# Reordering one pair of heads in a fused attention and soft-mixture kernel: transposes in another PSUM ring, V products and denominators at other places

## The chip, the cores and the metric

The kernel runs on one core of one Trainium2 chip. The metric is the device time of one execution in microseconds (us). A core has a matrix engine (PE, with its weight loads shown apart as PEld), a vector engine (DVE), an activation engine (ACT), a general engine (POOL) and a sync engine (SP). Each works through its own queue in order, and they meet at semaphores. PE writes its results to PSUM, which has eight banks of 512 float32 values in each of 128 partitions; DVE and ACT empty them.

## The reference

```python
def _attn_ref(q, k, v):                       # 8 batches, 12 heads, 448 tokens, 64 channels
    scores = scale * np.matmul(q, k.transpose(0, 1, 3, 2))
    m = np.max(scores, axis=-1, keepdims=True)
    e = np.exp(scores - m)
    attn = e / (np.sum(e, axis=-1, keepdims=True) + np.exp(-m) + 1e-09)
    return np.matmul(attn, v).astype(np.float32)

def _moe_ref(x, phi, w1, w2):                 # x: 3584 x 768, phi: 768 x 32, 8 experts of 4 slots
    logits = x @ phi
    d = np.exp(logits - logits.max(0, keepdims=True))
    d /= d.sum(0, keepdims=True) + 1e-09
    slot_input = (d.T @ x).reshape(E, S_per_e, D)
    for e in range(E):
        slot_out[e] = np.maximum(slot_input[e] @ w1[e], 0.0) @ w2[e]
    c = np.exp(logits - logits.max(1, keepdims=True))
    c /= c.sum(1, keepdims=True) + 1e-09
    return (c @ slot_out).astype(np.float32)
```

The attention's output, with its heads side by side, is the x of the second part. The dispatch weights d are normalised over all 3584 rows, so the experts can begin only when the last head is done.

## The kernel before

The 96 heads are worked as 48 pairs of heads of one batch: one head lies in partitions 0 to 63, the other in 64 to 127. Six pairs make a batch; three pairs make a group, whose q, k and v are loaded together. The loop of line 647 goes over the pairs s; each has two half chunks, y = 0 and y = 1, and hs = 2s + y counts them. Everything is written out by hand in the order in which each engine is to run it: the program is not reordered.

For one pair the work is this.

- `T(n)` (L237): 28 transposes of 64x64 turn q and k, six pairs ahead, into one PSUM tile. One copy, on ACT (L256) or on DVE (L258), brings them to one of seven buffers.
- `A` and `A1` (L269, L288): products of q against k, seven PSUM tiles a pair, three to four pairs ahead. DVE takes the maximum of each row (L278, L286, L293).
- `W2`, `W3` (L296, L306), once per group of three pairs: the maxima are turned (L300 to L303) and copied by ACT (L308), and ACT takes exp(-m) of them (L312, L315).
- `AB(n, i)` (L348), key blocks i = 0, 1, 2 of 128 keys: k against q (`scores`, L360), minus the maximum by a second product into the same bank (`less`, L363), and the exponential on ACT (L365). One tile of the row maxima (`A1`, L292) runs ahead of it and one behind. `Bk(n, 3, 1)` (L319) does the fourth block of 64 keys (L338, L341, exponential L344), with the `A` of L284 inside.
- `AV(n, i, qs)` (L386, L398): the exponentials against V, 65 columns a product; the last column of V is one, which gives the denominators. Query blocks 0 to 2 are wide products (24 a pair), query block 3 is narrow (8 a pair, half of the output partitions each). All 32 add up in one PSUM bank.
- `N1(n)` (L404): that bank is copied to SBUF, by ACT (L410) for pairs 0 to 43 and DVE after that. `N2(n)` (L413): DVE adds exp(-m) to the denominators (L419) and takes the reciprocal (L420), then POOL (pairs 0 to 43) or DVE multiplies (L424, L428, L429). `PX(n)` (L443) turns the result (L450) and ACT copies it (L456).
- `P(b)` (L463): per batch, the logits, their maxima, their exponentials and the running sum of the slots' inputs, cut into steps that the table `post` spreads over the half chunks of the next batch but one: logits (L476, L489, L493) in a half chunk y = 0, their transposes (L501, L503, and a subtraction on POOL, L508) in y = 1, the running maximum (L513, L514, L516) in y = 0, exponentials (L525, L530) in y = 0, slot sums (L544, L535, L558) in y = 1, and one more turn (L549) in y = 1.

PSUM is three rings of banks: psA with three (rows' maxima, the steps of P, and the transposes of pairs 8 and later), psB with four (scores for the exponentials, W2, PX, and the transposes of pairs 0 to 7), psV with one (the V products). A tile is given the bank that the ring's oldest tile left, and PE waits until that one has been read.

The order of a half chunk before, away from the start and the end:

- y = 0: blocks 0 and 1; the wide V products of key blocks 2 and 3 of the pair before; a step of P where there is one; the narrow V products of the pair before; N1 (and N2, where DVE does it all).
- y = 1: block 2; block 3; the transposes of pair s + 6; W2 and W3 in one pair of three; wide V products of key blocks 0 and 1; a step of P; PX of pair s - 2; N2.

Loads and the copies of V by POOL (L377) follow at the end of a pair. After the loop come the last pair's rest, the experts (L751 to L849) and the output (L851 to L866).

## Time and profile before

| | |
|---|---|
| time, three runs | 303.99, 305.38, 305.58 us; median 305.38 us |
| the profiled execution's own time | 304.84 us |
| its span, first to last instruction | 303.1 us |
| mean granted PE clock | 0.948 |
| busy: PE, DVE, ACT, POOL | 275.1, 254.4, 249.3, 184.8 us |
| row maxima on DVE (L293) | 254 of 616 ns mean, 139.9 us |
| exponentials on ACT (L365) | 272 of 576 ns mean, 131.2 us |
| copies of transposes, ACT (L256) and DVE (L258) | 20 of 924 ns, 27 of 616 ns |
| V products on PE (L398) | 1536, 64.5 us |

A line of a view has the engine, the line of the program, the operation, what it writes and reads, its shapes, and how many there were. In the timeline the first two numbers are the start and the duration of a run of like instructions, in microseconds from the first instruction; brackets at the end give the idle time of the engine before it and what ended that. The mean of a row is one instruction's own length; instructions of one engine overlap, so the starts tell more of the pace than the lengths. The window from 33 to 224 us is the part in which the transposes are still running beside everything else.

### The profile page before, as it was taken

Reading aid. Unit: us, or ns where it says so; the run is one execution under the profiler, and the core shown is the slowest. Engines: PE = TensorE matmul, PEld = TensorE weight load, DVE = VectorE, ACT = ScalarE, POOL = GpSimd, SP = SyncE. Lnnn points to the kernel's source line nnn. Section 1 sums busy time; section 2 is a strip of 40 time slices with the busy share of each in tenths; the row PEclk is TensorE's granted clock in tenths of the full one; section 3 lists DMA queues with packets and bytes.
Section 4 is the critical chain, followed back from the end, with each engine's and each line's share of the span. In section 5 each row is a group of like instructions: output and inputs, shape, how many; then the busy total and the mean of one; then the engine's idle time right before and its main releaser. Section 6 shows DMA issues by size and latency. Waiting matters only on the chain.

```text
span 303.1 us, 12159 instructions
## 1 busy us (share of the span) xinstructions
PE 275.1 (91%) x5097; PEld 159.3 (53%) x5097; DVE 254.4 (84%) x590; ACT 249.3 (82%) x551; POOL 184.8 (61%) x336
## 2 busy tenths in 40 slices
PE   7998999999999999999999999999999998994800
PEld 3344656566665666556656575656665455541100
DVE  7889999999999999989999999999999566447900
ACT  3567999999999999989999999999999995345800
POOL 8691986969596869866877778696747652000000
PEclk9599999999999999999999999999999999998555
DMA  7999899999999999999999999999846999909995
GB/s 130 143 149 202 124 206 208 203 199 174 186 179 195 163 198 161 200 190 155 117 202 144 191 195 208 159 204 205 138 54 107 133 151 247 336 29 347 440 410 233
DMA packets 49384, 57.69 MB, mean 190 GB/s; under 512 B 2865, under 2 KB 41521, under 8 KB 48945
## 3 DMA queue, kind: packets, MB, share of 16 engines
q0 software_dynamic: 45280, 42.29, 90.5%
q1 hardware_dynamic: 4048, 14.62, 12.2%
q8 instruction: 40, 0.66, 0.8%
q14 instruction: 16, 0.12, 0.1%
HBM read 88.18 MB, written 14.16 MB: 338 GB/s over the span
## 4 chain that ended last, share of the span: by engine, by line
PE 66%; DVE 15%; ACT 10%; issue 3%; POOL 0%; DVEq 0%; POOLq 0%
PE ps_av L398 14%; PE ps_a L292 9%; PE ps_b L360 7%; DVE R L293 6%; PE ps_b L363 6%; PE ps_t L252 6%; PE ps_b L338 4%; ACT R L344 3%; PE ps_x L450 2%; PE ps_b L341 2%; PE ps_o L803 2%; ACT R L256 2%; DVE R L278 2%; PE ps_so L774 2%; PE ps_h L758 2%
## 5 line engine op out<-in xcount | busy, mean ns | idle before, releaser
L293 DVE TENSOR_REDUCE R<-ps_a 128x1 bf16<-128x448 f32 x254 | 139.9, 616 | 5.6 <-PE ps_a L292 5.1
L365 ACT ACTIVATE R<-ps_b 128x448 bf16<-128x448 f32 x272 | 131.2, 576 | 0.5 <-PE ps_b L363 0.2
L292 PE MATMUL ps_a<-R 64*128 64x448 bf16 x254 | 82.8, 352 | 0.3 <-DVE R L278 0.2
L360 PE MATMUL ps_b<-R 64*128 64x448 bf16 x272 | 74.7, 353 | 1.1
L363 PE MATMUL ps_b<-mT,sel 64*128 64x448 bf16 x272 | 71.3, 350 | 0.1
L424 POOL TENSOR_TENSOR R<-ubuf,rec 128x384 bf16<-128x384 f32 x44 | 36.2, 822 | 50.0 <-DVE rec L420 21.8
L398 PEld LDWEIGHTS <-R 128*128 128x128 bf16 (+1 forms) x1536 | 50.6, 101 | 27.8 <-issue 23.7
L398 PE MATMUL ps_av<-R 128*128 128x65 bf16 (+1 forms) x1536 | 64.5, 196 | 0.0
L344 ACT ACTIVATE R<-ps_b 128x448 bf16<-128x448 f32 x64 | 36.1, 581 | 3.5 <-PE ps_b L341 3.5
L252 PEld LDWEIGHTS <-R 64*64 64x64 bf16 x1344 | 29.7, 111 | 12.4 <-issue 4.6
L456 ACT CAST R<-ps_x 128x512 bf16<-128x512 f32 x47 | 28.1, 599 | 6.5 <-PE ps_x L450 6.5
L252 PE MATMUL ps_t<-ident,R 64*64 64x64 bf16 x1344 | 30.9, 195 | 0.6
L286 DVE TENSOR_REDUCE R<-ps_a 128x1 bf16<-128x448 f32 x48 | 29.7, 619 | 0.6 <-PE ps_a L284 0.6
L363 PEld LDWEIGHTS <-sel 64*128 64x128 bf16 x272 | 21.8, 94 | 15.3 <-issue 5.5
L292 PEld LDWEIGHTS <-R 64*128 64x128 bf16 x254 | 23.8, 94 | 11.0 <-issue 1.0
L410 ACT COPY ubuf<-ps_av 128x455 f32<-128x455 f32 x44 | 25.1, 571 | 0.6 <-POOL R L429 0.4
L256 ACT COPY R<-ps_t 128x896 bf16<-128x896 bf16 x20 | 18.5, 924 | 5.5 <-PE ps_t L252 5.1
L338 PE MATMUL ps_b<-R 64*64 64x448 bf16 (+1 forms) x112 | 22.0, 378 | 0.0
L278 DVE TENSOR_REDUCE R<-ps_a 128x1 bf16<-128x448 f32 x34 | 19.0, 618 | 2.5 <-PE ps_a L275 2.2
L341 PE MATMUL ps_b<-mT,sel 64*64 64x448 bf16 (+1 forms) x112 | 20.8, 357 | 0.0
L429 POOL TENSOR_TENSOR R<-ubuf,rec 128x128 bf16<-128x128 f32 x44 | 17.5, 398 | 3.7
L360 PEld LDWEIGHTS <-R 64*128 64x128 bf16 x272 | 17.3, 94 | 4.7 <-issue 0.3
(139 smaller groups left out, 442.6 us busy)
## 6 DMA issues: line engine op xcount, KB each, us to landing
W<-in_moe_w_dram POOLq DMA_DIRECT2D x22, 768.0 KB, 10.1
R<-in_v_dram POOLq DMA_DIRECT2D x32, 192.0 KB, 4.8
out_dram<-W SPq DMA_DIRECT2D x2, 2688.0 KB, 12.1
R<-in_q_dram POOLq DMA_DIRECT2D x14, 336.0 KB, 7.8
R<-in_k_dram POOLq DMA_DIRECT2D x14, 336.0 KB, 8.7
wd<-in_moe_w_dram POOLq DMA_DIRECT2D x8, 384.0 KB, 9.9
R<-wd SPq DMA_DIRECT2D x8, 384.0 KB, 7.8
R<-in_moe_w_dram POOLq DMA_DIRECT2D x2, 768.0 KB, 8.0
```

The source lines that it names most:

```text
L252: nc.tensor.transpose(ps[r, a, c:c + 64], src[r, pl, tok * D:(tok + 1) * D], ident[r, r])
L286: nc.vector.reduce_max(top(n, i), ps[:, 0:S], axis=AX.X)
L292: nc.tensor.matmul(ps[:, 0:S], t[r, 0, i * 128:(i + 1) * 128], t[r, 1, :], start=True, stop=True)
L293: nc.vector.reduce_max(top(n, i, hl), ps[:, 0:S], axis=AX.X)
L338: nc.tensor.matmul(outs[hl], t[rs[hl], 1, cols], t[rs[hl], 0, :], start=True, stop=False)
L344: nc.scalar.activation(e, p[:, 0:S], AF.Exp, scale=scale)
L360: nc.tensor.matmul(ps[hl][:, 0:S], t[rs[hl], 1, cols], t[rs[hl], 0, :], start=True, stop=False)
L363: nc.tensor.matmul(ps[hl][:, 0:S], sel[rs[hl], pl:pl + 1].to_broadcast([64, 128]), mT[mg(n)][rs[hl], :], start=False, stop=True)
L365: nc.scalar.activation(e[:, hl, :], ps[hl][:, 0:S], AF.Exp, scale=scale)
L398: nc.tensor.matmul(o, eT[n, i, hl][:, qc], vp[g % 2][:, 2 * pl + hl, i, 0:W65], start=(i == 0 and u == 0 and hl == 0), stop=(i == 3), skip ...
L424: eng.tensor_mul(x[:, 0:3, c:c + 128].rearrange("p i (h d) -> p i h d", h=2), u[:, 0:6, 0:D].rearrange("p (i h) d -> p i h d", h=2), rec[: ...
L456: nc.scalar.copy(xT[:, pb, :], pss[0])
```

## The change

Five things change, all of them in order or place; no arithmetic is added or left out.

1. The transposes take their PSUM tile from psB for all pairs, not from psA for pair 8 and later. The copy goes to ACT for the second pair of a group (pl == 1), before for the first.
2. In y = 1 the transposes come between block 2 and block 3, before behind block 3.
3. In y = 0 the eight narrow V products come between block 0 and block 1, before at the end of the half chunk. N1 follows the wide V products at once, ahead of the step of P.
4. N2 becomes N2a (the sum, L419) and N2b (reciprocal and multiplications). Where POOL multiplies, N2a stands between the transposes and block 3, and N2b behind block 3, ahead of W2, W3 and the step of P; before, both came at the end of the half chunk behind PX.
5. In y = 1 the step of P comes before the wide V products, before after them.

The first two and a half pairs (`early`) keep their own order of blocks.

```diff
--- before.py
+++ after.py
@@ -236,13 +236,12 @@
 
         def T(n):
             g, pl = divmod(n, NP)
-            tp, tg = (psB, "b") if n < 8 else (psA, "a")
             t = qk_t[n % NQK]
-            ps = tp.tile([128, 2, S], BF16, tag=tg, name="ps_t")
+            ps = psB.tile([128, 2, S], BF16, tag="b", name="ps_t")
             for a in range(2):
                 if n == 0 and a:
                     nc.scalar.copy(t[:, 0, :], ps[:, 0, :])
-                    ps = tp.tile([128, 2, S], BF16, tag=tg, name="ps_t")
+                    ps = psB.tile([128, 2, S], BF16, tag="b", name="ps_t")
                 src = nat["qk"[a], g]
                 for tok in range(7):
                     for hl in range(2):
@@ -252,7 +251,7 @@
                         nc.tensor.transpose(ps[r, a, c:c + 64], src[r, pl, tok * D:(tok + 1) * D], ident[r, r])
             if n == 0:
                 nc.vector.tensor_copy(t[:, 1, :], ps[:, 1, :])
-            elif n < 8 or pl == 0:
+            elif n < 8 or pl == 1:
                 nc.scalar.copy(t, ps)
             else:
                 nc.vector.tensor_copy(t, ps)
@@ -410,13 +409,17 @@
             (nc.scalar.copy if on_pool(n) else nc.vector.tensor_copy)(u, src)
             us[n] = u
 
-        def N2(n):
-            g, pl = divmod(n, NP)
+        recs = {}
+
+        def N2a(n):
+            recs[n] = psm.tile([128, 7], F32, tag="rec", name="rec", bufs=3)
+            nc.vector.scalar_tensor_tensor(recs[n], us[n][:, :, D], 1e-9, ec[mg(n)][:, n % NP, :],
+                                           op0=ALU.add, op1=ALU.add)
+
+        def N2b(n):
             b, pb = divmod(n, PB)
-            u = us[n]
+            u, rec = us[n], recs[n]
             eng = nc.gpsimd if on_pool(n) else nc.vector
-            rec = psm.tile([128, 7], F32, tag="rec", name="rec", bufs=3)
-            nc.vector.scalar_tensor_tensor(rec, u[:, :, D], 1e-9, ec[mg(n)][:, pl, :], op0=ALU.add, op1=ALU.add)
             nc.vector.reciprocal(rec, rec)
             x = xb[b % 2]
             c = pb * 128
@@ -656,46 +659,51 @@
                     Bk(s, 2 * y + 1)
                     warm(int(hs < 2), S)
                     As(1)
-                elif s < NPAIR:
-                    AB(s, 2 * y)
-                    if y:
-                        Bk(s, 3, 1)
-                    else:
-                        AB(s, 1)
+                elif y == 0:
+                    AB(s, 0)
+                    for i in range(4):
+                        AV(s - 1, i, [3])
+                    AB(s, 1)
+                else:
+                    AB(s, 2)
+                    if s < NPAIR - 6:
+                        T(s + 6)
+                    if on_pool(s - 1):
+                        N2a(s - 1)
+                    Bk(s, 3, 1)
                 if hs < 5:
                     T(hs + 3)
                 if y == 0:
-                    if 0 <= s - 1:
+                    if s:
                         for i in (2, 3):
                             AV(s - 1, i, range(3))
+                        if early:
+                            for i in range(4):
+                                AV(s - 1, i, [3])
+                        N1(s - 1)
+                        if not on_pool(s - 1):
+                            N2a(s - 1)
+                            N2b(s - 1)
                 else:
-                    if 2 <= s < NPAIR - 6:
-                        T(s + 6)
+                    if s and on_pool(s - 1):
+                        if early:
+                            N2a(s - 1)
+                        N2b(s - 1)
                     g = (s + 1) // 3
                     if (s + 1) % 3 == 0 and g < NG:
                         W2(g + 1)
                         W3(g + 1)
-                    if s < NPAIR:
-                        for i in (0, 1):
-                            AV(s, i, range(3))
-                if 2 * s + y in post:
-                    post[2 * s + y]()
+                if hs in post:
+                    post[hs]()
+                if y:
+                    for i in (0, 1):
+                        AV(s, i, range(3))
                 if hs == 2 * (NPAIR - 2) + 1:
                     nc.vector.reduce_max(fold, ident.rearrange("p (i s) -> p s i", i=4), axis=AX.X)
                 if y and 0 <= s - 2 < NPAIR - 2 and s - 2 != n6:
                     PX(s - 2)
                 if hs == 2 * n6 + 4:
                     PX(n6)
-                if y == 0:
-                    if 0 <= s - 1:
-                        for i in range(4):
-                            AV(s - 1, i, [3])
-                        N1(s - 1)
-                        if not on_pool(s - 1):
-                            N2(s - 1)
-                else:
-                    if 0 <= s - 1 and on_pool(s - 1):
-                        N2(s - 1)
                 As(last_)
                 if hs == 1:
                     W2(1)
@@ -733,7 +741,8 @@
         AV(n, 3, range(4))
         load_second(0, 4)
         N1(n)
-        N2(n)
+        N2a(n)
+        N2b(n)
         PX(n - 1)
         last[0]()
         last[1]()
```

## The prediction

> **What bounds the kernel now.** The granted clock and the engines' busy time by window come first: they say whether the attention part has one bound.
>
> ```profile
> 33.00:224.00 191.00, 188.86 (x3823) 118.00 (x3818) 181.82 (x421) 183.53 (x421) 146.44 (x260) 1.00 1.14 180
> ```
>
> The columns are the stretch, then busy microseconds of PE, PEld, DVE, ACT and POOL, the granted clock, the DMA share and GB/s. The clock is full (1.00). DVE is idle for 191.00 - 181.82 = 9.2 us and ACT for 191.00 - 183.53 = 7.5 us. Three engines run almost full, so no reordering that leaves their work alone can win much more than the 7.5 us. PE's 188.86 says little: records of matmuls overlap, and a matmul that starts late hides behind the end of the one before. So I read PE by starts, in the timeline of one pair and the beginning of the next:
>
> ```profile
> 141.80 0.55 PE L360 MATMUL ps_b<-R 64*128 64x448 bf16 x2
> 142.00 0.54 PE L363 MATMUL ps_b<-mT,sel 64*128 64x448 bf16 x2
> 142.19 0.54 PE L292 MATMUL ps_a<-R 64*128 64x448 bf16 x2
> 142.38 0.80 PE L360 MATMUL ps_b<-R 64*128 64x448 bf16 x2
> 142.84 0.53 PE L363 MATMUL ps_b<-mT,sel 64*128 64x448 bf16 x2
> 143.04 0.35 PE L292 MATMUL ps_a<-R 64*128 64x448 bf16 x1
> 143.32 0.79 PE L398 MATMUL ps_av<-R 128*128 128x65 bf16 x20
> ...
> 144.71 0.38 PE L338 MATMUL ps_b<-R 64*64 64x448 bf16 x2
> ...
> 144.93 0.35 PE L341 MATMUL ps_b<-mT,sel 64*64 64x448 bf16 x2
> 145.12 0.63 PE L252 MATMUL ps_t<-ident,R 64*64 64x64 bf16 x28
> 145.68 0.54 PE L398 MATMUL ps_av<-R 128*128 128x65 bf16 x12
> ...
> 146.95 0.54 PE L360 MATMUL ps_b<-R 64*128 64x448 bf16 x2
> 147.14 0.54 PE L363 MATMUL ps_b<-mT,sel 64*128 64x448 bf16 x2
> 147.51 0.35 PE L292 MATMUL ps_a<-R 64*128 64x448 bf16 x1
> ```
>
> A step of two 448-column matmuls takes 0.19 (142.00 to 142.19). Three kinds of step are longer. First, L360 of the second key block at 142.38: 0.46 to the next line instead of 0.19; it waits for a psB bank. Second, L292 at 147.51 comes 0.37 after L363 instead of 0.19: the second row-maximum product waits for a psA bank, which DVE frees. The third is the transposes' wait for psA, seen in another pair; below it stands a pair without transposes:
>
> ```profile
> 154.98 0.35 PE L341 MATMUL ps_b<-mT,sel 64*64 64x448 bf16 x2
> 155.45 0.63 PE L252 MATMUL ps_t<-ident,R 64*64 64x64 bf16 x28
> ```
>
> ```profile
> 228.86 0.35 PE L341 MATMUL ps_b<-mT,sel 64*64 64x448 bf16 x2
> 229.14 0.54 PE L398 MATMUL ps_av<-R 128*128 128x65 bf16 x12
> ```
>
> Here the transposes start 0.47 after L341, against 0.19 at 145.12. The pattern repeats every six pairs (one batch), in 29.5 us (the transposes of 145.12 come again at 174.64). Over the six pairs from 92 to 121 us I summed each step's excess over its smallest: psA wait in the second key block 0.81, psA wait of the transposes 0.43, psB wait of the second key block 0.37, psA wait in the third block 0.13. Sum 1.74 us of 29.5. The other two engines around the end of that pair:
>
> ```profile
> 145.60 0.70 ACT L344 ACTIVATE R<-ps_b 128x448 bf16<-128x448 f32 x1
> 146.47 0.59 ACT L456 CAST R<-ps_x 128x512 bf16<-128x512 f32 x1 [0.18 <-PE ps_x L450]
> ```
>
> ```profile
> 146.57 0.16 DVE L419 SCALAR_TENSOR_TENSOR rec<-ubuf,ec 128x7 f32<-128x7 f32 x1
> 146.76 0.20 DVE L420 RECIPROCAL rec<-rec 128x7 f32<-128x7 f32 x1
> 146.88 2.17 DVE L293 TENSOR_REDUCE R<-ps_a 128x1 bf16<-128x448 f32 x4
> ```
>
> ACT runs dry before L456; DVE's reciprocal starts 0.19 after the sum it reads, the reduce only 0.12 after the reciprocal.
>
> **The change, part by part** (times per pair, PE by starts).
>
> Narrow products between key blocks 0 and 1. Now: 0.20 + 0.19 + 0.19 + 0.19 + 0.19 + 0.28 + 0.72 = 1.96 for blocks 0 and 1 and twenty V products. After: 0.20 + 0.19 + 0.28 (last L292 to a V product, as at 143.04), 0.25 for eight narrow products (where other work splits the twenty, they take 0.25 and the wide twelve 0.38), then 0.20 + 0.19 + 0.28 + 0.38. Sum 1.97, so no own cost. But block 1 starts 0.53 after block 0's last L292 rather than beside it, which is longer than any of the waits in block 1: the 0.81 and the 0.37 per six pairs should go. What is late next: the narrow products read the fourth key block's exponential of the pair before, now 0.67 after a pair's start instead of some 1.7.
>
> Transposes to psB and ahead of the fourth key block. Their wait for psA goes (0.43 per six). Now L341 to transposes is 0.19 and L341 to the V products in a pair without transposes is 0.28 (229.14), so the new order costs 0.09 a pair, 0.54 per six; bounds 0 (the transposes' own 0.56 may shrink by as much when 64x64 products follow them) and 0.09; I take 0.09, the row of the same neighbours. In psB nine tiles a pair instead of eight go round four banks. Counting four back: the transposes wait for the first exponential of block 1, the fourth block for the second, block 0's second scores for the transposes' copy, block 1's second scores for L456 as now. With exponentials 0.42 apart (four at 146.96 last 1.85) all but the last two are over 0.5 us early. No DMA moves: V's copies and the loads stay behind the pair. The copy on ACT moves from the group's first pair to its second, same count and about 0.79 of ACT each (0.94 long), against 0.53 on DVE. That is the pair where ACT now runs dry, but it is followed by the pair with the mT copy and two small exponentials (0.75 of ACT together). The copy also stands before the fourth block's exponential now, so that one, L456 and the next pair's first exponentials are behind it.
>
> Sum and reciprocal apart. A small operation behind an independent one starts about 0.1 earlier than behind its own input (0.12 against 0.19 above), so DVE gains 0 to 0.09 a pair; I count 0.05 in DVE's load. The Trainium skill, "VectorE: DVE Perf Modes", section "The DRAIN you can't avoid", says that the next operation does not start until the pipe has emptied, which would make the split worth nothing; the reduce at 146.88, before the reciprocal's end at 146.96, disagrees, and my sum by that rule would move by under 1 us. N2b passes the batch steps on POOL's queue: once in six pairs a subtraction waits 1.5 us more (0.82 + 0.28 + 0.40), and its reader comes three half chunks later. Cost nothing; without that cover at most 7 x 1.5 us.
>
> Copy of the V products (N1) ahead of the batch steps, and batch steps ahead of the next V products. Both are only order; N1 (0.42 to the next ACT operation) fits into the 0.68 that the logits' 24 products take, and psV's one bank is free earlier. Cost 0, gain 0 to 0.2 per six; I take 0.
>
> New waits. With waits gone, PE needs 29.5 - 1.74 + 0.54 + 0.13 left over = 28.4 per six. DVE's load per pair is 7 x 0.53 + 0.26 + 0.53 for a copy on two of three = 4.51 or 3.98, against PE's 4.40. In the pair with the running maximum DVE has 0.43 more and PE 0.15: it falls 0.39 behind and the banks cover about 0.25 of that. In the pair with both the ACT copy and the batch's exponentials ACT has 3.87 + 0.79 + 0.73 = 5.4 against PE's 5.1, and the mT pair follows; I price that at 0.4 per six, the other small deficits at 0.15. New waits 0.7 in all, bounds 0 and 1.7.
>
> Sum: 28.4 + 0.7 = 29.1, so 0.42 gained per six pairs. 39 pairs have transposes: 6.5 x 0.42 = 2.7 us. In the last six pairs the eight narrow products cover part of block 1's wait, but ACT is busy throughout there (3.46 of about 3.7 a pair); 0.5 us. The tail after 252 us waits for no DMA landing in the list of waits and moves along. 304.84 - 3.2 = 301.6 for the profiled execution (303.1 span and 1.7 around it), which stands 0.5 below the median of 305.38; so about 302.2.
>
> **The rivals.**
> 1. Slower by ACT's queue. The ACT copy stands ahead of the fourth block's exponential, and the narrow products wait for that. By my walk that exponential ends 0.55 into the next pair in a copy pair, and the products come at 0.67: 0.12 of room. For: ACT is only 7.5 us idle in 191. Against: the pair that had the copy till now has 0.4 more room. If ACT lags by 0.57 at each of the 13 copies, 0.45 each time, 5.9 us: 304.84 - 3.2 + 5.9 = 307.5, median 308. It decides from 0.25 a copy upward (3.2 / 13).
> 2. About even, by array shapes. The order has one more change between 64x128, 128x64 and 128x128 products per pair. The step from wide to narrow V products costs 0.72 - 0.38 - 0.25 = 0.09; if each change costs that and my 0.28 does not hold all of it, 48 x 0.09 = 4.3 us: 305.9, median 306.4. Against: 147.51 to 147.79 and 143.04 to 143.32 show 0.28 for that step in either order. The Trainium skill, "TensorEngine Tiling (Array Packing)", section "Key Properties", states that changing the tiling mode drains the engine; the 0.28 in place of 0.19 agrees.
> 3. Same, because waits only move: DVE's 0.39 deficits and ACT's together eat 1.1 per six. 304.8, median 305.3.
> 4. More: new waits 0.1 per six. 28.5 per six gives 1.0 x 6.5 + 0.5 = 7 us: 297.8, median 298.4; ACT's idle time allows no more.
>
> **How the numbers follow.** Three runs spread over 1.6 us, so 0.5% (1.5 us) is about what can be told from no change. Chances: the forecast with its new waits between 0.4 and 1.0 (median 300.3 to 304.0) 0.42; rival 4 0.15; rival 3 0.18; rival 2 0.08; rival 1 0.17. Faster by over 0.5% (under 303.9): 0.15 + 0.41 = 0.56. Within 0.5%: rival 3, half of rival 2 and the forecast's edge, 0.21. Slower: 0.23. The range 298.8 to 307.2 leaves out a tenth at each end; the forecast's own range is 300.3 to 304.0.
>
> **What would show it.** Right: L363 to L292 in block 1 back to 0.19, no L360 of 0.80 there, transposes right after the third block's last L292, the batch's period 28.9 to 29.3, ACT's idle time before L456 gone. Wrong: narrow products starting over 0.3 after block 0's last L292 (rival 1), or all steps at their shortest and the period still 29.5 (rival 2), or L292's waits moved into the third block (rival 3). A shift in the tail, or a granted clock below 1.00 before 250 us, would make the prediction wrong for a reason outside it.

## The result and the profile after

The changed kernel takes 301.71 us (median of four executions, 300.40 to 305.08) against 304.94 us before on the same chip: a ratio of 0.988 (95% interval 0.984 to 0.992), so 1.2% faster. The same kernel measured a second time, with six executions beside seventeen of the kernel before, gave 301.89 against 305.36 us, 0.988 (0.983 to 0.992). The ratios leave out slow executions such as the one of 305.08 us, the medians do not. The forecast was 302.2.

The profile taken with the first measurement is of its 305.08 us execution, in which PE stood 3.4 us for its own instructions between the first PX and the 40th; the readings below are therefore of the second measurement's profile (span 299.8 us), and the odd one comes back in the last section.

First the windows over the attention part, with the columns that were explained for the kernel before:

```profile
33.00:224.00 191.00, 189.03 (x3872) 109.89 (x3865) 180.21 (x425) 184.21 (x424) 146.39 (x260) 1.00 1.13 181
```

The clock is 1.00 here as before. ACT is idle for 6.8 us instead of 7.5, and it now does slightly more than the same stretch of the program. DVE is idle for 10.8 instead of 9.2. The three engines remain almost equally full, so what was won in this stretch is a matter of order.

Next the timeline of PE over one pair of the changed kernel, the pair that answers to the one shown of before (start, duration, engine, line, operation, tiles):

```profile
141.78 0.55 PE L359 MATMUL ps_b<-R 64*128 64x448 bf16 x2
141.98 0.53 PE L362 MATMUL ps_b<-mT,sel 64*128 64x448 bf16 x2
142.17 0.35 PE L291 MATMUL ps_a<-R 64*128 64x448 bf16 x1
142.44 0.32 PE L397 MATMUL ps_av<-R 128*64 128x65 bf16 x8
...
142.70 0.55 PE L359 MATMUL ps_b<-R 64*128 64x448 bf16 x2
142.90 0.54 PE L362 MATMUL ps_b<-mT,sel 64*128 64x448 bf16 x2
143.09 0.35 PE L291 MATMUL ps_a<-R 64*128 64x448 bf16 x1
143.37 0.53 PE L397 MATMUL ps_av<-R 128*128 128x65 bf16 x12
...
143.84 0.55 PE L359 MATMUL ps_b<-R 64*128 64x448 bf16 x2
144.04 0.54 PE L362 MATMUL ps_b<-mT,sel 64*128 64x448 bf16 x2
144.23 0.35 PE L291 MATMUL ps_a<-R 64*128 64x448 bf16 x1
144.51 0.56 PE L251 MATMUL ps_t<-ident,R 64*64 64x64 bf16 x24
...
144.97 0.36 PE L337 MATMUL ps_b<-R 64*64 64x448 bf16 x2
145.17 0.35 PE L340 MATMUL ps_b<-mT,sel 64*64 64x448 bf16 x2
145.45 0.54 PE L397 MATMUL ps_av<-R 128*128 128x65 bf16 x12
145.83 0.39 PE L453 MATMUL ps_x<-ident,R 128*128 128x128 bf16 x4
146.15 0.63 PE L359 MATMUL ps_b<-R 64*128 64x448 bf16 x2
```

The second key block now starts at 142.70, 0.53 after the first one's last L291, and it has no wait left: L359, L362 and L291 follow at 0.20 and 0.19, where before the step behind L360 took 0.46 (142.38) and the step to L292 0.37 (147.51) in the pairs shown. The transposes (144.51) stand right behind the third block's L291 (0.28, a change of shape), and nothing waits there. The whole pair takes 4.37 us (141.78 to 146.15); a pair of the same kind took 4.54 and 4.57 before (from the first PX at 166.46 to those at 171.00 and 175.57).

A batch of six pairs takes 28.90 us in the stretch without other disturbance, by the first PX of one pair to that of the sixth behind it (151.29 to 180.19, and 180.19 to 209.09), against 29.52 before (151.50 to 181.02, and 181.02 to 210.54). The six steps are 4.94, 5.07, 4.68, 4.37, 4.37 and 5.47. By the same excess over the smallest step as in the forecast, 0.53 us of waits is left in the six, against 1.74 before.

ACT's dry spell ahead of PX's copy is gone too. From the list of waits of the kernel before (in all, times, longest), and from the groups of the changed kernel, whose last columns are the idle time in front and what ended most of it:

```profile
ACT R L456 <- PE ps_x L450: 6.5, 16, 1.5
```

```profile
L459 ACT CAST R<-ps_x 128x512 bf16<-128x512 f32 x47 | 28.8, 613 | 1.8 <-PE ps_x L453 0.7
```

6.5 us of waiting for the products of PX became 0.7.

Where did the time go between the two profiled spans, 303.1 and 299.8? To the first PX: 34.0 before, 34.2 after. From there to the 40th: 191.5 and 189.6. From there to the end: 77.6 and 76.1. So 1.9 us came from the 39 pairs and 1.5 from the tail. In the 39 pairs PE stands 0.7 us for "issue" before and 0.4 after (so the profile calls time in which an engine waits for nothing that it shows). After, it also stands once for a load: the transposes of k wait for k itself.

```profile
38.87 0.34 PE L251 MATMUL ps_t<-ident,R 64*64 64x64 bf16 x10 [1.16 <-DMA R<-in_k_dram]
```

Without these waits the 39 pairs gained 2.8.

### The profile page after: what moved, and what is told of

Read it like the earlier page. It is cut to its first block, busy times and chain, and to the rows that moved or that the text cites. A ratio compares the mean times of both kernels' runs of the same rounds, so it can differ in the third digit from the quotient of the medians.

```text
span 303.3 us, 12152 instructions
## 1 busy us (share of the span) xinstructions
PE 274.6 (91%) x5096; PEld 149.6 (49%) x5097; DVE 251.8 (83%) x590; ACT 248.0 (82%) x551; POOL 184.6 (61%) x336
## 4 chain that ended last, share of the span: by engine, by line
PE 72%; DVE 11%; issue 5%; ACT 4%; DMA 2%; POOL 1%; DVEq 0%; ACTq 0%; POOLq 0%
PE ps_av L397 15%; PE ps_a L291 11%; PE ps_b L359 8%; PE ps_b L362 7%; PE ps_t L251 7%; DVE R L292 4%; PE ps_x L453 3%; PE ps_b L337 3%; PE ps_b L340 3%; DMA R<-in_k_dram 2%; PE ps_o L812 2%; PE ps_so L783 2%; PE ps_s L547 2%; PE ps_h L767 2%; DVE W L820 2%
## 5 line engine op out<-in xcount | busy, mean ns | idle before, releaser
L292 DVE TENSOR_REDUCE R<-ps_a 128x1 bf16<-128x448 f32 x254 | 140.5, 617 | 6.2 <-PE ps_a L291 5.6
L291 PE MATMUL ps_a<-R 64*128 64x448 bf16 x254 | 90.2, 355 | 0.3
L359 PE MATMUL ps_b<-R 64*128 64x448 bf16 x272 | 73.2, 354 | 0.0
L362 PE MATMUL ps_b<-mT,sel 64*128 64x448 bf16 x272 | 70.6, 349 | 0.1
L397 PE MATMUL ps_av<-R 128*128 128x65 bf16 (+1 forms) x1536 | 67.2, 196 | 2.1 <-issue 2.1
L427 POOL TENSOR_TENSOR R<-ubuf,rec 128x384 bf16<-128x384 f32 x44 | 36.1, 820 | 51.0 <-DVE rec L423 14.5
L251 PEld LDWEIGHTS <-R 64*64 64x64 bf16 x1344 | 26.0, 112 | 21.6 <-issue 20.5
L251 PE MATMUL ps_t<-ident,R 64*64 64x64 bf16 x1344 | 31.8, 197 | 1.7 <-issue 1.3
L459 ACT CAST R<-ps_x 128x512 bf16<-128x512 f32 x47 | 28.8, 613 | 2.2 <-PE ps_x L453 1.2
L285 DVE TENSOR_REDUCE R<-ps_a 128x1 bf16<-128x448 f32 x48 | 29.7, 619 | 1.0 <-PE ps_a L283 1.0
L362 PEld LDWEIGHTS <-sel 64*128 64x128 bf16 x272 | 23.8, 95 | 12.5 <-issue 2.2
L291 PEld LDWEIGHTS <-R 64*128 64x128 bf16 x254 | 23.7, 93 | 9.6 <-issue 1.1
L409 ACT COPY ubuf<-ps_av 128x455 f32<-128x455 f32 x44 | 25.7, 585 | 0.2 <-issue 0.2
L453 PE MATMUL ps_x<-ident,R 128*128 128x128 bf16 x192 | 18.7, 219 | 0.0
```

What stands on the lines that cost most here:

```text
L251: nc.tensor.transpose(ps[r, a, c:c + 64], src[r, pl, tok * D:(tok + 1) * D], ident[r, r])
L285: nc.vector.reduce_max(top(n, i), ps[:, 0:S], axis=AX.X)
L291: nc.tensor.matmul(ps[:, 0:S], t[r, 0, i * 128:(i + 1) * 128], t[r, 1, :], start=True, stop=True)
L292: nc.vector.reduce_max(top(n, i, hl), ps[:, 0:S], axis=AX.X)
L359: nc.tensor.matmul(ps[hl][:, 0:S], t[rs[hl], 1, cols], t[rs[hl], 0, :], start=True, stop=False)
L362: nc.tensor.matmul(ps[hl][:, 0:S], sel[rs[hl], pl:pl + 1].to_broadcast([64, 128]), mT[mg(n)][rs[hl], :], start=False, stop=True)
```

## The experiments

The theory of the forecast: two edits remove PE's waits for PSUM banks in the second key block and before the transposes, the split of the denominators gives DVE a little, the rest is order; and what is left waits on ACT and DVE. The rival readings were that one edit alone carries the whole, that the waits merely move, that the array's shapes eat the gain, and that something not in the forecast (the start of the weights' loads, the tail) makes the difference. All ratios are against the kernel before on the same chip; "six pairs" is the batch period from the trace, and "tail" the time from the 40th pair's PX to the end.

| kernel | ratio (95% interval) | median us | six pairs us | tail us |
|---|---|---|---|---|
| before | 1 | 304.8 to 305.4 | 29.52 | 77.6 |
| changed, second time | 0.988 (0.983 to 0.992) | 301.89 | 28.90 | 76.1 |
| narrow products put back | 0.992 (0.989 to 0.995) | 302.19 | 29.14 to 29.28 | 76.9 |
| transposes put back | 0.990 (0.986 to 0.993) | 302.22 | 29.40 to 29.46 | 76.0 |
| denominators put back | 0.988 (0.984 to 0.992) | 301.65 | 29.15 | 76.4 |
| narrow products alone | 0.992 (0.989 to 0.995) | 303.06 | 29.53 | 76.4 |
| transposes alone | 0.996 (0.992 to 0.999) | 303.71 | 29.41 to 29.47 | 77.6 |
| transposes in psB, behind block 3 | 0.989 (0.986 to 0.992) | 301.71 | 29.23 to 29.29 | |
| batch steps put back | 0.982 (0.978 to 0.986) | 299.74 | 28.90 | |
| copy on ACT a pair earlier | 0.978 (0.975 to 0.980) | 298.27 | 28.64 | 76.0 |
| V products together | 1.048 (1.043 to 1.052) | 320.07 | 31.2 to 32.8 | |
| weights spread | 0.986 (0.984 to 0.989) | 300.89 | 28.90 | |
| weights late (one execution) | | 321.94 | 28.90 at 72 to 130 us | |

The intervals of several of these overlap. What differs by less than about 0.5% is read from the period in the trace, not from the time.

**The changed kernel once more**, unaltered.

> The changed kernel unaltered, for a profile without the waits of 0.5 to 1.2 us for 'issue' that the profile of after shows between 39 and 136 us (about 5 us in all). Theory (the steady order of the six-pair pattern, 28.90 us in the undisturbed part of that profile, is what the change brings, and the issue waits are one execution's bad luck): median 300.5 to 302, and at most two such waits in the profile, as in the profile of before. Rival (a faster pair runs ahead of the fetching of PE's instructions, so the waits belong to the change): the same number of such waits again, about eight, and a median over 302.

This is the profile read above. It holds 0.4 us of waits for "issue" where the first profile holds 3.4, so the waits are not a fixed cost of the change.

**Each part put back into the changed kernel.** Narrow products:

```diff
-                    for i in range(4):
-                        AV(s - 1, i, [3])      # between the two key blocks
...
-                        if early:
-                            for i in range(4):
-                                AV(s - 1, i, [3])
+                        for i in range(4):
+                            AV(s - 1, i, [3])  # behind the wide ones, as before
```

> The changed kernel with the eight narrow V products back behind the wide ones (block 0 and block 1 adjacent again). Theory (the narrow products cover the waits for psA and psB in block 1): L362 to L291 in block 1 goes from 0.19 back to 0.3 or more in most pairs, the six-pair period from 28.9 to 29.4 to 29.9 us, the time up by 3 to 6 us, 304 to 307. Rival (the gain is from the transposes and the denominators; block 1 would have been free of waits once psA no longer holds the transposes): period at 28.9 or below, time within 1 us of the changed kernel.

The waits of the second block came back: L362 to L291 takes 0.20 to 0.39 there, and in two of the six pairs the step behind L359 takes 0.30 and 0.48 instead of 0.19, a wait for a psB bank. The period is 0.24 to 0.38 longer than the changed kernel's, less than expected (29.4 to 29.9), and the times can't be told apart.

Transposes, with the ring, the place and the pair in which ACT copies:

```diff
-            ps = psB.tile([128, 2, S], BF16, tag="b", name="ps_t")
+            tp, tg = (psB, "b") if n < 8 else (psA, "a")
+            ps = tp.tile([128, 2, S], BF16, tag=tg, name="ps_t")
...
-            elif n < 8 or pl == 1:
+            elif n < 8 or pl == 0:
...
+                    # T(s + 6) again behind block 3
```

> The changed kernel with the transposes as before: psA from pair 8 on, behind block 3, ACT's copy for the first pair of a group. Theory: the wait of the transposes for psA comes back (0.43 us per six pairs), PE's 0.06 for the new order goes, and block 1's psA wait stays small as the narrow products cover it; period 29.1 to 29.4, time up by 1 to 3 us. Rival (the narrow products alone are the change): time within 0.7 us of the changed kernel. Second rival (the ring is what matters most): up by more than 3.5 us.

The transposes' own wait for psA is back: over six pairs 0.47, 0.25, 0.34, 0.25, 0.23 and 0.46 from the step before them, where 0.19 is the smallest. The period is 0.50 to 0.56 longer, the largest loss of the three in the trace and a little more than expected, though its time can't be told from the changed kernel's. Three things were put back at once here. The kernel with ACT's copy a pair earlier (28.64, below) differs from this one in the ring and the place alone; beside it, these two are worth 0.8 a period.

Denominators, N2a and N2b again together at the end of the pair:

```diff
-                        N2a(s - 1)             # y = 0
...
-                        N2b(s - 1)             # y = 1, ahead of the V products
...
+                if y and s and on_pool(s - 1):
+                    N2a(s - 1)
+                    N2b(s - 1)
```

> The changed kernel with the sum, the reciprocal and the multiplications together at the end of the half chunk y = 1, behind PX. Theory (DVE has 0 to 0.09 us a pair from the split, and is not PE's bound in most pairs): the time 0 to 1 us up, period 28.9 to 29.1. Rival (the split and its earlier place are worth what they save on DVE, since DVE sets the pace): up by 2 us or more.

The period is 0.25 longer: in three of the six pairs L362 to L291 in the second block takes 0.26 to 0.31, since DVE frees psA later. In time it makes no difference that can be seen. The run undoes the split and the earlier place together.

**One part alone, put into the kernel before.** The narrow products only (the first diff turned round):

> The kernel before with one edit: the eight narrow V products between block 0 and block 1. Theory (they cover both waits of block 1, 0.81 + 0.37 of the 1.74 us per six pairs, and the transposes' wait for psA stays): L363 to L292 in block 1 at 0.19 in nearly every pair; but as the row with the transposes as before had a period of 29.4 with block 1 free of waits, part of it moves to the transposes' and the fourth block's wait for psA: period 29.3 to 29.5 (29.52 before), time down by 1 to 2.5 us, of which about 1 us behind the last transposes. Rival (block 1's waits were the whole loss): period 28.7 or less, the full 3.5 us.

The time is 0.8% lower, but the six pairs take 29.53, as before. The second block indeed has no wait left. PE in the pair with the running maximum:

```profile
153.57 0.52 PE L363 MATMUL ps_b<-mT,sel 64*128 64x448 bf16 x2
...
154.38 0.35 PE L341 MATMUL ps_b<-mT,sel 64*64 64x448 bf16 x2
154.85 0.63 PE L252 MATMUL ps_t<-ident,R 64*64 64x64 bf16 x28
```

L341 to the transposes is 0.47 here, and over six pairs these steps are 0.33, 0.25, 0.40, 0.47, 0.25 and 0.41: 0.97 of excess, where the kernel before has 0.43. What the second block no longer waits for is waited for by the next tile of the psA ring, the transposes. Its faster tail (76.4 against 77.6) is the part of its gain that can be seen in the trace.

The transposes only:

> The kernel before with one edit: transposes in psB, between block 2 and block 3, ACT's copy for the second pair of a group. Theory (psA with seven tiles a pair in place of eight lets DVE run further behind, so most of block 1's waits shrink too): period 29.1 to 29.3, time down by 1.5 to 3 us. Rival (the two edits are independent, so this one is worth 0.43 - 0.36 per six pairs at most): period 29.4 or more, time within 1 us of before.

Here it is the other way about. The transposes have no wait, and the second block's have grown:

```profile
155.32 0.52 PE L363 MATMUL ps_b<-mT,sel 64*128 64x448 bf16 x2
155.92 0.35 PE L292 MATMUL ps_a<-R 64*128 64x448 bf16 x1
```

0.60 from L363 to L292, and 0.20 to 0.44 in the other pairs of a batch: 1.07 of excess (0.28, 0.59, 0.35, 0.35, 0.44, 0.20 from 120 to 145 us), where the kernel before has 0.81. The period gains 0.05 to 0.11, as the rival expected (29.4 or more), though its reason, that the two edits are independent, does not hold: neither edit alone shortens the period by more than about 0.1, both together with the denominators as before gain 0.37 (29.15, the run "denominators put back"), and the changed kernel gains 0.62. What the traces show fits one shortage, of psA tiles that DVE has not yet read: one edit moves most of the wait to the other place.

**Ring or place?** The transposes stay in psB, but stand behind the fourth key block as before:

```diff
-                    if s < NPAIR - 6:
-                        T(s + 6)
                     # blocks 2 and 3 of the pair
+                    if s < NPAIR - 6:
+                        T(s + 6)
```

> The changed kernel with the transposes in psB but behind block 3, where they were before. Tells the ring from the place. Theory (the ring is what frees psA; the place costs PE nothing, 0.28 + 0.46 + 0.19 + 0.28 against 0.28 + 0.21 + 0.19 + 0.56): the plain pair stays at 4.37 to 4.40, period 28.9 to 29.1, time within 1 us of the changed kernel. Rival (the place matters, since it splits the stretch of PE without row maxima between block 3 and the next pair, in which DVE runs dry): period 29.2 or more, and reduces that wait for PE at the start of pairs.

The plain pair is 4.37 as in the changed kernel, so the place itself costs PE nothing. The period is 0.33 to 0.39 longer, the rival's 29.2 or more, by waits: in the logits pair the step behind the fourth block's scores takes 0.47 instead of 0.21, since the row tile of L283 inside that block waits for the bank that DVE's maximum of the logits (L496) frees; the second scores of block 0 come 0.36 instead of 0.20 after the first in the next pair; and L362 to L291 in block 1 takes 0.41 instead of 0.19 in the one behind it. The rival's reason, reduces that wait for PE, does not show: DVE stands 2.6 us for L291 from 33 to 226 us in both kernels. So the place is worth 0.33 to 0.39; what the ring is worth alone was not isolated, as the kernel with the transposes put back differs from this one in ACT's copy too.

**The batch steps back behind the wide V products**, in y = 1:

```diff
-                if hs in post:
-                    post[hs]()
...                                             # AV(s, 0), AV(s, 1)
+                if hs in post:
+                    post[hs]()
```

> The changed kernel with the step of the batch behind the next wide V products again, in the half chunks y = 1 (the logits' transposes, the slot sums, the last turn). Theory (pure order: 0.38 later for the slot sums, nobody waits): period 28.8 to 29.0, time within 1 us. Rival (the slot sums' evacuation by DVE, 0.31, lands 0.38 later in a pair where DVE has no room): the pair with the slot sums goes from 5.07 to 5.3 or more, period 29.1 or more.

The period is 28.90, the same, as the theory had it. The interval of the time overlaps with the changed kernel's; the forecast's "only order" stands, and no more is shown.

**ACT's copy of the transposes in the group's first pair**, as before, with all else changed:

```diff
-            elif n < 8 or pl == 1:
+            elif n < 8 or pl == 0:
```

> The changed kernel with ACT's copy of the transposes for the first pair of a group again, so that the pair before the mT copy has none and the pair after it has one. Theory (the copy of 0.79 us stands two pairs ahead of the mT copy and has a pair to drain): ACT's queue is less full in the pair with the mT copy; the wait of 0.09 in the pair with the logits goes; period 28.8 to 29.0, time within 1 us. Rival (the pair after the mT copy is still behind by 0.75 and gets 0.79 more): block 0 or the narrow products wait there by 0.2 to 0.5, period 29.2 to 29.9.

This beats both kernels: 298.27 us, 0.978 (0.975 to 0.980), an interval that lies below the changed kernel's. Neither the theory (28.8 to 29.0, the time within 1 us) nor the rival expected it. The reason can be followed in the timeline. First ACT and DVE of the changed kernel around the logits:

```profile
145.44 0.95 ACT L255 COPY R<-ps_t 128x896 bf16<-128x896 bf16 x1
...
148.83 0.67 ACT L409 COPY ubuf<-ps_av 128x455 f32<-128x455 f32 x1
149.25 0.42 ACT L492 COPY lb<-ps_l 128x128 f32<-128x128 f32 x1
...
149.70 0.29 DVE L496 TENSOR_REDUCE cm<-ps_l 128x4 f32<-128x128 f32 x1 [0.94 <-ACT lb L492]
```

ACT copies the transposes (0.95) in the pair just ahead of the one with the logits, so its queue is late by the time it reaches N1 (L409) and the copy of the logits (L492). DVE has the maximum of the logits next in its queue and stands still for 0.94. With it everything behind it comes late, its own copy of transposes and the reduce of L285 among them, and one pair further on PE pays:

```profile
151.83 0.52 PE L362 MATMUL ps_b<-mT,sel 64*128 64x448 bf16 x2
152.25 0.35 PE L291 MATMUL ps_a<-R 64*128 64x448 bf16 x1
```

0.42 instead of 0.19. With the copy a pair earlier, first ACT and DVE, then PE at the same place:

```profile
146.02 0.55 ACT L409 COPY ubuf<-ps_av 128x455 f32<-128x455 f32 x1
146.44 0.30 ACT L492 COPY lb<-ps_l 128x128 f32<-128x128 f32 x1
...
146.76 0.29 DVE L496 TENSOR_REDUCE cm<-ps_l 128x4 f32<-128x128 f32 x1 [0.51 <-ACT lb L492]
...
148.57 0.16 DVE L416 SCALAR_TENSOR_TENSOR rec<-ubuf,ec 128x7 f32<-128x7 f32 x1
148.64 0.62 DVE L285 TENSOR_REDUCE R<-ps_a 128x1 bf16<-128x448 f32 x1
```

```profile
149.20 0.53 PE L362 MATMUL ps_b<-mT,sel 64*128 64x448 bf16 x2
149.39 0.35 PE L291 MATMUL ps_a<-R 64*128 64x448 bf16 x1
```

DVE stands for 0.51 and L291 comes after 0.19. Over the run the list of waits has this one seven times, in this order for the changed kernel, the copy a pair earlier, and the kernel before:

```profile
DVE cm L496 <- ACT lb L492: 6.0, 7, 1.0
```

```profile
DVE cm L496 <- ACT lb L492: 3.4, 7, 0.5
```

```profile
DVE cm L493 <- ACT lb L489: 1.7, 7, 0.5
```

The period is 0.26 shorter, 1.7 us over 6.5 batches. That is somewhat over half of the 1.0% (3 us) between the two ratios. Of the 3.1 us between the two profiled spans (299.8 and 296.7) another 1.2 is the changed kernel's wait for the load of k at 38.87, which this profile does not have; the waits for "issue" are 0.4 in both. Whether the load's wait is also what stands between the medians isn't settled.

**What remains in PE: V products all together.** Several steps of a pair pay for changes of shape. Here all the wide V products of a pair run in the next pair's y = 0 and PX goes to y = 0, so that y = 1 has no 128x128 products but W2's and the batch's (the flag that starts a bank's sum moves to the narrow products, which are now the first):

```diff
-                        for i in (2, 3):
+                        for i in range(4) if 3 <= s - 1 else (2, 3):
                             AV(s - 1, i, range(3))
...
-                if y:
+                if y and not 3 <= s < NPAIR - 1:
                     for i in (0, 1):
                         AV(s, i, range(3))
...
-                if y and 0 <= s - 2 < NPAIR - 2 and s - 2 != n6:
+                if 0 <= s - 2 < NPAIR - 2 and y == int(s < 5):
                     PX(s - 2)
```

> The changed kernel with all 24 wide V products of a pair in one run behind block 1 of the next pair (before: twelve there and twelve behind block 3 of its own), and PX behind them, so that the half chunk y = 1 has no 128x128 products but W2's and the batch's. Theory (a change between 64x128 and 128x128 products costs 0.09 on PE, and PE is close to its shortest sequence in the changed kernel): PE's plain pair goes from 4.37 to 4.2, the six-pair period from 28.90 to 28.3 to 28.7, held there by DVE's 28.2 to 28.5; the time 1 to 4 us below the changed kernel. Rival (DVE and ACT already set the pace, or 1.07 us of PE without row maxima starves DVE): period 28.9 or longer, time the same or up to 2 us longer.

It is 4.8% slower, with 31.2 to 32.8 us for six pairs where the theory expected 28.3 to 28.7. The rival had the sign right and was far too small. ACT and then PE where the pair with W2 and W3 meets the next:

```profile
144.39 0.54 ACT L343 ACTIVATE R<-ps_b 128x448 bf16<-128x448 f32 x1
144.83 0.53 ACT L307 CAST mT<-ps_m 128x448 bf16<-128x448 f32 x1
```

```profile
144.64 0.55 PE L359 MATMUL ps_b<-R 64*128 64x448 bf16 x2
145.41 0.37 PE L362 MATMUL ps_b<-mT,sel 64*128 64x448 bf16 x2 [0.23 <-ACT mT L307]
```

The twelve V products and PX (0.38 + 0.32 of PE) had stood between the fourth key block and the next pair's first. Without them L362 comes 0.77 after L359, because it reads mT, which ACT is still copying behind the fourth block's exponential. In the other pairs the narrow products wait for that exponential: the eight take 0.31 to 0.92 instead of 0.25, split as here:

```profile
154.91 0.29 PE L398 MATMUL ps_av<-R 128*64 128x65 bf16 x6
155.67 0.22 PE L398 MATMUL ps_av<-R 128*64 128x65 bf16 x2 [0.47 <-ACT R L343]
```

DVE runs dry too; its waits for L291 in this kernel, and in the changed one:

```profile
DVE R L292 <- PE ps_a L291: 17.8, 41, 1.8
```

```profile
DVE R L292 <- PE ps_a L291: 3.5, 12, 0.5
```

Most of these come at one place, behind the 24 wide products and PX, 1.05 us of PE (146.80 to 147.85) in which no tile for DVE is made:

```profile
146.80 0.90 PE L398 MATMUL ps_av<-R 128*128 128x65 bf16 x24
...
147.85 0.36 PE L291 MATMUL ps_a<-R 64*128 64x448 bf16 x1
```

```profile
148.25 1.16 DVE L292 TENSOR_REDUCE R<-ps_a 128x1 bf16<-128x448 f32 x2 [0.43 <-PE ps_a L291]
```

34 of the 41 waits, 15.6 of the 17.8 us, are for the first L291 behind such a run: the mechanism that the rival of this run named. Beside it PE stands 2.9 us for the fourth block's exponential, which is the wait of the forecast's first rival, with its cover taken away instead of ACT made late, and 1.4 us for mT. How much of the 4.8% each is worth was not separated.

**Do the weights' loads hold up PE's instructions?** In the 305.08 us execution PE waited for "issue" several times. The loads of the experts' weights run beside the attention; they were put at other pairs:

```diff
-        half_at = {s: i for i, s in enumerate((1, 4, 7, 10, 13, 16, 22, 25, 28, 31, 34))}
+        half_at = {s: i for i, s in enumerate((1, 5, 9, 13, 17, 21, 25, 28, 31, 34, 37))}      # spread
+        half_at = {s: i for i, s in enumerate((21, 23, 25, 27, 29, 31, 33, 35, 37, 39, 41))}   # late
```

> The changed kernel with the eleven weight loads begun at pairs 1, 5, 9, 13, 17, 21, 25, 28, 31, 34 and 37 in place of 1, 4, 7, 10, 13, 16, 22, 25, 28, 31 and 34: a quarter less of them in the first half, and the last ones three pairs later. Theory (the packets of PE's instructions start earlier and PE waits less for them, and the experts do not reach the last weights sooner than these land): at most one wait for issue over 0.4 us in the loop, median 0.5 to 2 us below the changed kernel, 300 to 301.4, and a smaller spread. Rival (the waits come from the loads of q, k and v, which stay): no change in the waits, time within 0.7 us of the changed kernel; if the last weights land late, 1 us or more longer, with a wait of the experts' first products.

> The changed kernel with the eleven weight loads issued at pairs 21 to 41 in place of 1 to 34, so that the DMA queues carry less from about 33 to 130 us and more from 135 to 240 us. Theory on the issue waits (16 KB packets of PE's instructions queue behind the kernel's own loads; PE waits where a packet begins too late): in the first window each instruction packet starts within 70 PE rows of a multiple of 256 and no wait of over 0.4 us for issue follows, in the second the starts are later (over 80 rows) and waits of 0.4 to 1.2 us appear. Rival (the waits belong to places in the program, such as the slot sums at 130 us): the same places wait, whatever the loads do. The experts may wait for the late weights, so the total is no measure here.

Spread out, PE still stood three times (0.38 at 110.5, 0.67 at 117.5, 0.59 at 149.0), more than was expected, and the time can't be told from the changed kernel's: this decides nothing. With the loads late, the stretch from 38 to 130 us, which has few of them, shows no such wait and 28.9 us for each six pairs (71.9, 100.8, 129.7). The one wait is at 148.6 (0.42). The kernel as a whole is much slower (321.94 in its one execution), for other reasons: POOL stands 5.7 us before a copy of V whose load has not landed (224.54), PX stands up to 4.5 us for POOL's multiplication (L427), and the tail takes 89.7 instead of 76.1.

## Why the prediction was right, point by point

**Waits in the second block and of the transposes (1.74 per six, 0.13 to be left over): right in place and size.** PE without its remaining waits needs 28.90 - 0.53 = 28.37; the forecast had 28.4. What the step did not say is that its terms don't add singly: it listed four waits as four sums that each edit removes, and the runs with one edit show that the wait goes to the other place (0 and about 0.1 gained alone, 0.37 together, 0.62 with the denominators' edit). The three waits for psA behave as one shortage, of tiles that DVE had not yet read. The 0.37 for psB is different: it goes with the narrow products alone, where the step behind L360 is 0.20 in every pair.

**Narrow products between the blocks, "no own cost", 1.97 after 1.96: mis-sized by 0.1 a pair.** It is 2.07 (141.77, where the pair's first matmul starts, to 143.84). The term that failed is the twelve wide products, put at 0.38. They take 0.38 where PX follows (145.45 to 145.83) and 0.47 where scores follow (143.37 to 143.84). The second rival's 0.09 for a change of shape is thus real at this place: 128x128 followed by 64x128. The Trainium skill, "TensorEngine Tiling (Array Packing)", section "Key Properties", says that changing the tiling mode drains the engine; 0.47 beside 0.38 agrees. The change from the narrow 128x64 products to 64x128 scores costs as much, but was already in the forecast's 0.25: the eight start in twos 0.03 to 0.05 apart, and the scores 0.13 after the last two (142.57 to 142.70).

**Transposes ahead of the fourth block, 0.09 a pair: the wrong end of the bounds.** From the third block's last L291 to the V products it takes 1.22 (144.23 to 145.45), where before it took 1.25 (144.43 to 145.68). The transposes take 0.46 with 64x64 products behind them where they took 0.56 with V products behind: the gain that the forecast named and took as nothing. With the term before, the pair comes to 4.37 where 4.40 was forecast. Two errors of 0.1 cancel, which is luck.

**Split of sum and reciprocal, 0.05 a pair: right in size, for split and place together.** Put back, the period is 0.25 longer, 0.04 a pair. In the timeline above the reduce of L285 starts 0.07 after the sum (148.57 to 148.64); the reciprocal had to wait 0.19. The sum lasts 0.16, so the reduce begins before it has ended. The Trainium skill, "VectorE: DVE Perf Modes", section "The DRAIN you can't avoid", has the next operation wait until the pipe is empty, but adds that one that is not held starts earlier, which the forecast left out; the 0.07 is such an earlier start, so the trace does not disagree.

**Order of N1 and of the batch steps, 0: right as far as it can be seen** (28.90 with the steps put back). N1's place was not tried alone.

**ACT's copy in the second pair: right on the fourth block's exponential, wrong on where it costs.** The narrow products never waited (0.28 behind L291 in the steady pairs), so the first rival did not come. But the new waits were put into the pair with the copy and the batch's exponentials (0.4 of 0.7), and there is none there. They are in the logits pair (0.09: the second scores of block 0 wait for the transposes' bank, which ACT's copy frees at 146.39) and in the next (0.23), there by a chain that the forecast did not follow: copy on ACT, N1, copy of the logits, DVE's maximum of the logits, DVE's reduces, PE. 0.21 is with the running maximum, where 0.14 (0.39 less 0.25) was forecast. In sum 0.53 instead of 0.7.

**The sum.** 0.62 gained per six instead of 0.42, so 4.0 for 6.5 batches instead of 2.7; 1.5 in the tail instead of 0.5. That would be 5.5 us, and it is 3.2 in the profiled spans and 3.2 to 3.5 in the medians. The period of 28.90 holds only in undisturbed batches. The first two batches behind the first PX were shorter already before (28.44 and 29.25) and gained only 0.3 each, the load of k aside, which cost 1.2. The third gained nothing (29.54 against 29.52), which no one row explains. So the time came out near the forecast partly by luck: a larger gain met losses that the forecast had no term for.

**The third rival** (waits only move, the time stays) is what each edit does to the period when alone. The fourth (new waits of 0.1 only, 28.5 per six, 298.4 us) is nearly what the kernel with the copy a pair earlier does: 28.64 and 298.27. In it DVE still stands for 0.5 at the logits.

## What to carry to other kernels

Waits for banks of one ring at several places are one shortage: an edit that ends one of them may only send it to the next tile in the ring, so remove them together, and don't call an edit worthless because it gained nothing alone. When a copy can go to either of two in-order queues or to another pair, follow what stands behind it through the next engine's queue too; 0.95 us of ACT ahead of the logits cost DVE 0.4 and PE 0.2 a whole pair later, and moving it back was worth another 1%. Ask of every block of products what it covers: twelve V products and PX that looked free to move hid an exponential and a copy, and gathered into one run they left DVE without tiles; moving them cost 4.8%.

## What was not expected of the hardware

PE waits for its own instructions in the middle of the attention. The profile's page counts 40 packets on an instruction queue (packets, MB, share):

```profile
q8 instruction: 40, 0.66, 0.8%
```

That is 16 KB each, and in the trace about one for each 256 of PE's instructions, each matmul and each weight load counted. In the 305.08 us execution of the changed kernel, the chain of waits has these:

```profile
69.83 0.50 issue
...
76.37 0.44 issue
...
83.06 1.03 issue
...
90.73 0.39 issue
```

In PE's timeline one of them splits the 28 transposes in two:

```profile
82.62 0.44 PE L251 MATMUL ps_t<-ident,R 64*64 64x64 bf16 x16
84.10 0.31 PE L251 MATMUL ps_t<-ident,R 64*64 64x64 bf16 x8 [1.03 <-issue]
```

The packets there began 125 to 150 PE instructions past a multiple of 256 (at 67.9, 74.4, 81.9 and 88.6 us), and each was followed by such a wait, which ended 2.2 to 2.6 us after the packet began. The same holds over all fourteen profiles: of the 21 waits above 0.15 us that are put to "issue" between the first PX and 230 us, every one ends 2.2 to 2.6 us after a packet began, and every one stands before the same instruction of a block, the one 194 past a multiple of 256. So these are waits for the packet: PE reaches this place before it is there. In the stretch with few loads, in the kernel with the weights late, the packets began at most 68 past a multiple or within the last 66 before the next, and no wait followed; at the wait behind it (148.6) the packet began 111 past. A late packet is not enough by itself, nor an early one safe: in the kernel before, one that began 78 past was followed by 0.74 (at 131.9), and in the second profile of the changed kernel one that began 101 past by none. That the kernel's own loads delay the packets is what the quiet stretch suggests; spreading the loads did not end the waits, so it is not shown. The waits differ between executions of one kernel: 0.4 us in one profile of the changed kernel and 3.4 in another, as much as the change itself is worth.
